# V of batch 0 with two tokens to a partition: odd and even keys in separate 64-row score and value matmuls

## The chip, the cores and the metric

The kernel runs on one core of one Trainium2 chip. The metric is the device time of the whole program in microseconds (us), as a median of several runs.

## The reference

Chunked attention with memory, followed by a two-layer network. There are 4 batches, 8 heads, 768 tokens and 64 elements to a head; a chunk has 32 queries, which see 16 keys to the left, their own 32 and 8 to the right, and 8 memory keys:

```python
for c in range(nc):                       # 24 chunks of 32 queries
    q_c = q[:, :, c_start:c_end]
    k_full = np.concatenate([mem_k, k[:, :, l_start:r_end]], axis=2)
    v_full = np.concatenate([mem_v, v[:, :, l_start:r_end]], axis=2)
    scores = scale * np.matmul(q_c, k_full.transpose(0, 1, 3, 2))
    a = np.exp(scores - np.max(scores, axis=-1, keepdims=True))
    a = a / (np.sum(a, axis=-1, keepdims=True) + 1e-09)
    out[:, :, c_start:c_end] = np.matmul(a, v_full)
...
x = out.transpose(0, 2, 1, 3).reshape(3072, 512)
h = x @ w_in                              # 512 -> 2048
s = np.sin(alpha * h)
return (h + s * s / (alpha + 1e-09)) @ w_out
```

## The kernel before, in words

**Tiles.** Three chunks make a block of 96 queries (QW), so a head has NJ = 8 blocks. The keys of a block are a window of 128 rows: 64 tokens from 16 before the block, 8 memory keys, 56 more tokens. Scores are computed transposed, keys on partitions and queries along the free dimension, so that exp gives the weights of the value matmul directly. A column of ones behind V gives the sum of a row; `normed` (L384) takes its reciprocal and multiplies on DVE, and `turned` (L396) transposes the result on PE, copies it on DVE or ACT and so fills xT, the input of the network. `half_tile` (L456) is the first matmul of the network (L462), `sine` (L473) its sine on ACT, `finish` (L487) the sum on DVE, `second` (L496) the second matmul (L500).

**Stages.** Stage -1, here called the front, does attention of batch 0 and nothing else. Stage i (0 to 3) does the network of batch i, with attention of batch i + 1 in between. The five strings of WORDS (L22) are a hand-kept list of words, one string to a stage, and every engine gets its instructions in the order of the words. In the front: `y`, `z` are filler matmuls on zeros; `a4A` casts a loaded piece of q or k (pieces 0 to 3 are k of two heads each, 4 to 7 q) on ACT (A) or DVE (V); `k1`, `l1` transpose k or q of two heads on PE (`turn`, L308) and `K1V`, `L1A` copy them out; `s10` computes scores of heads 2 and 3 in the first half of the sequence (`u_scores`, L348), `v10` the values (`u_values`, L373); `t10`, `T10` the turn with its copy on DVE or ACT; `V024` loads V of heads 2 and 3 of batch 0; `C` stands for constants, `m0` puts the memory values into V's tile, `I27` loads columns of w_in, `p`/`P` start the first network tile early.

**Batch 0.** A call of `u_scores` handles two heads (e = 0, 1) and four blocks. The two heads lie on partitions 0 to 63 and 64 to 127, so their matmuls have 64 rows each. Masking is added by a matmul of `mrow` and `mind` (L351) into the same PSUM banks, then eight score matmuls follow (L359, 96 columns each) and one exp on ACT (L366). `u_values` has eight matmuls (L378) of 128 rows and 65 columns. V's tile `vw` holds one token on a partition; `load_v` (L197) fetches it with 256-byte pieces in two DMAs a call, from POOL's queue (L209, L216, L205 for the first block). POOL issues its DMAs in order, as do SP (k of the first six heads, then outputs) and ACT (q of the first six heads). The memory values are cast (L827) and spread over the blocks on DVE (L225).

PE runs its instructions in order; every matmul that is printed below has a weight load (LDWEIGHTS) of its own ahead of it.

## Time and profile before

| | |
|---|---|
| median of 3 runs | 215.37 us (214.87 to 215.49) |
| the profiled execution, by the clock outside | 214.11 us |
| its span, first to last instruction | 212.0 us |
| PE busy | 203.1 us (96%) |
| DVE, ACT, POOL busy | 139.9, 142.8, 100.8 us |
| first network matmul (L462) | 23.48 us after the span's start |
| bytes moved by DMA | 27.82 MB in 95853 packets |

How to read the rows. A row of the timeline is: start, duration (both in us), engine, line, operation, out<-in, shapes, count, and in brackets how long the engine was idle before and what ended it. PE is the matmul, PEld the weight load, DVE the vector engine, ACT the scalar engine, POOL the engine that issues most loads. A name with q (ACTq, SPq) is the engine's sequencer, here with the DMAs that it issues. The busy time by windows gives for a stretch of time the busy us and the number of instructions of each engine. A row of the DMA table is queue, packets, MB, and the time of the packets as a share of 16 engines' time; an issue row ends with the us from issue to landing. "issue" as the reason of a wait means that nothing in the profile explains it.

### The profile page before, as it was taken

How to read it: one execution, taken by the hardware profiler on the slowest of the kernel's cores; microseconds unless marked ns; L12 is line 12 of the kernel's file. 1: busy time of each engine (PE TensorE's matmuls, PEld its weight loads, DVE VectorE, ACT ScalarE, POOL GpSimd, SP SyncE). 2: the span in 40 equal slices, each digit the busy share in tenths (PEclk: the TensorE clock that was granted, in tenths of full speed). 3: DMA queues.
4: the chain of work that ended last, by engine and by line, in shares of the span. 5: the costliest groups of instructions: out<-in, count | busy, mean ns of one | idle time of the engine just before them, and what ended most of it. 6: DMA issues, size and time to landing. Idle time of an engine off the chain costs nothing.

```text
span 212.0 us, 4567 instructions
## 1 busy us (share of the span) xinstructions
PE 203.1 (96%) x1759; PEld 117.6 (55%) x1781; DVE 139.9 (66%) x211; ACT 142.8 (67%) x228; POOL 100.8 (48%) x142
## 2 busy tenths in 40 slices
PE   7798899999999999999999999999999999999994
PEld 7566555655455555555456555554555555554443
DVE  4788788999352669957675659887347189964011
ACT  2698798978838479978827299878755188891110
POOL 8988607498696395119894048960000023300000
PEclk9999999999999999999999999999999999999999
DMA  5999999999999999999998259999244400000312
GB/s 163 327 156 145 209 208 204 204 164 177 151 167 128 172 128 128 103 148 147 158 186 137 68 126 125 160 173 126 103 105 108 136 0 3 2 0 0 152 49 99
DMA packets 95853, 27.82 MB, mean 131 GB/s; under 512 B 84808, under 2 KB 92376, under 8 KB 95832
## 3 DMA queue, kind: packets, MB, share of 16 engines
q0 software_dynamic: 69152, 13.64, 85.9%
q1 hardware_dynamic: 25720, 12.68, 30.3%
q10 hardware_dynamic: 960, 1.21, 1.7%
q8 instruction: 14, 0.23, 0.5%
q14 instruction: 7, 0.06, 0.1%
HBM read 29.66 MB, written 6.29 MB: 170 GB/s over the span
## 4 chain that ended last, share of the span: by engine, by line
PE 77%; DVE 8%; ACT 5%; issue 4%; DMA 3%; POOL 1%; SPq 1%; DVEq 0%
PE ps L500 39%; PE ps L462 28%; DVE gT L489 3%; DMA kq_f<-in_k_dram 3%; PE ps L448 3%; DVE s L485 3%; PE ps L419 2%; ACT u L477 2%; DVE x_blk L388 2%; PE ps L313 1%; PE ps L400 1%; ACT qT L333 1%; POOL s L485 1%; ACT s L482 1%; PE ps L359 1%
## 5 line engine op out<-in xcount | busy, mean ns | idle before, releaser
L500 PE MATMUL ps<-w_out_sb,gT 128*128 128x512 bf16 (+2 forms) x382 | 86.9, 370 | 1.3 <-issue 0.3
L462 PE MATMUL ps<-xT,w_in_sb 128*128 128x384 bf16 x512 | 86.4, 326 | 0.6 <-DVE gT L489 0.3
L489 DVE SCALAR_TENSOR_TENSOR gT<-s,inv_alpha,ps 128x768 bf16<-128x768 f32 x64 | 63.1, 1012 | 11.9 <-POOL s L485 5.3
L462 PEld LDWEIGHTS <-w_in_sb 128*128 128x128 bf16 x512 | 49.6, 98 | 35.5 <-issue 2.3
L477 ACT ACTIVATE u<-ps,alpha_sb 128x768 f32<-128x768 f32 x64 | 56.6, 894 | 18.2 <-PE ps L462 17.9
L500 PEld LDWEIGHTS <-gT 128*128 128x128 bf16 x400 | 36.6, 98 | 37.8 <-DVE gT L489 0.2
L485 POOL TENSOR_TENSOR s<-u 128x768 f32<-128x768 f32 x11 | 17.9, 1632 | 65.5 <-ACT u L477 54.5
L433 ACT ACTIVATE pt<-ps,biasm 128x256 bf16<-128x256 f32 x72 | 27.1, 488 | 10.5 <-PE ps L419 10.5
L507 DVE COPY o_sb<-ps 128x512 f32<-128x512 f32 (+1 forms) x15 | 10.1, 678 | 28.4 <-PE ps L500 26.5
L485 DVE TENSOR_TENSOR s<-u 128x768 f32<-128x768 f32 x24 | 22.9, 953 | 7.3 <-ACT u L477 7.3
L482 ACT ACTIVATE s<-u 128x768 f32<-128x768 f32 x29 | 24.2, 841 | 0.5
L388 DVE TENSOR_TENSOR x_blk<-ps,rinv 96x512 bf16<-96x512 f32 x32 | 22.0, 687 | 1.1
L507 ACT COPY o_sb<-ps 128x512 f32<-128x512 f32 (+1 forms) x10 | 5.6, 561 | 22.3 <-PE ps L500 22.3
L387 DVE RECIPROCAL rinv<-ps 96x8 f32<-96x8 f32 x32 | 6.4, 199 | 13.4 <-PE ps L448 12.7
L209 POOL DMA_DIRECT2D vw<-in_v_dram x13 | 11.9, 912 | 6.6 <-PE ps L400 5.5
L216 POOL DMA_DIRECT2D vw<-in_v_dram x13 | 13.3, 1024 | 3.3 <-DMA vw<-in_v_dram 3.0
L275 POOL DMA_DIRECT2D kst<-in_k_dram x16 | 12.1, 758 | 1.7 <-DMA vw<-in_v_dram 0.9
L269 POOL DMA_DIRECT2D kst<-in_k_dram x16 | 11.7, 731 | 1.9 <-DMA vw<-in_v_dram 1.2
L282 POOL DMA_DIRECT2D q_bf<-in_q_dram x12 | 10.7, 911 | 0.0
L448 PEld LDWEIGHTS <-pt 128*128 128x128 bf16 x192 | 8.2, 97 | 4.2 <-ACT pt L433 0.3
L403 ACT COPY xT<-ps 128x384 bf16<-128x384 bf16 x10 | 4.9, 496 | 7.7 <-PE ps L400 7.7
L448 PE MATMUL ps<-vw,pt 128*128 128x65 bf16 x192 | 8.9, 193 | 0.0
(83 smaller groups left out, 139.0 us busy)
## 6 DMA issues: line engine op xcount, KB each, us to landing
out_dram<-o_sb SPq DMA_DIRECT2D x23, 256.0 KB, 2.7
q_bf<-in_q_dram POOLq DMA_DIRECT2D x12, 128.0 KB, 7.0
kq_f<-in_k_dram SPq DMA_DIRECT2D x3, 384.0 KB, 6.0
kq_f<-in_q_dram ACTq DMA_DIRECT2D x3, 384.0 KB, 8.5
w_in_sb<-in_moe_w_in_dram POOLq DMA_DIRECT2D x1, 1152.0 KB, 12.6
vw<-in_v_dram POOLq DMA_DIRECT2D x7, 128.0 KB, 7.8
vw<-in_v_dram POOLq DMA_DIRECT2D x8, 112.0 KB, 8.0
kst<-in_k_dram POOLq DMA_DIRECT2D x14, 64.0 KB, 5.9
```

Source lines behind the costliest of these rows:

```text
L216: nc.gpsimd.dma_start(vw[72:128, c0:hi, 0:D], win(vflat, base + QW * c0 + 48, hi - c0, 56))
L275: nc.gpsimd.dma_start(kst[72:72 + n, j, :].rearrange("p (h d) -> p h d", d=D), k[b, :, QW * j + 48:QW * j + 48 + n, :].rearrange("h p d -> ...
L388: nc.vector.tensor_tensor(out=x_blk[:].rearrange("p g e d -> p e g d"), in0=otv[0:QW, :, :, 0:D], in1=rinv[:].unsqueeze(3).to_broadcast([Q ...
L433: nc.scalar.activation(pt[:, 0:H * QW].rearrange("p (g e c) -> p g e c", g=2, e=4)[:, :, :, 32 * m:32 * m + 32], sc[:, :, 0:4 * QW].rearra ...
L448: nc.tensor.matmul(otv[:, e, hp, :], pt[:, QW * i:QW * i + P], vws[b % 2][:, 2 * hp + e, j, 0:D + 1],)
L462: nc.tensor.matmul(t["hT"][:, hf, 0:HALF], w_in_sb[:, kt, P * t["ft"]:P * t["ft"] + P], t["xT"][:, kt, HALF * hf:HALF * hf + HALF], start= ...
L477: nc.scalar.activation(t["u"][:], t["hT"][:, :, 0:HALF], ACTF.Sin, scale=alpha_sb[:, ft:ft + 1])
L482: nc.scalar.activation(s2[:], u[:], ACTF.Square)
L485: e.tensor_tensor(out=s2[:], in0=u[:], in1=u[:], op=ALU.mult)
L489: nc.vector.scalar_tensor_tensor(out=gT[:, ft, :].rearrange("p (e c) -> p e c", e=2), in0=t["s2"][:], scalar=inv_alpha[:, ft:ft + 1], in1= ...
L500: nc.tensor.matmul(o[:, c0:c1], gT[:, ft, P * s:P * s + P], w_out_sb[:, ft, c0:c1], start=(ft == 0), stop=(ft == FT - 1),)
L507: copier(state["engines"][state["o"] % len(state["engines"])])(o_sb[:, c0:c1], o[:, c0:c1])
```

## The change

V of batch 0 is stored with two consecutive tokens on one partition, and two neighbouring blocks (ab = 0, 1) lie side by side: one on partitions 0 to 63, the other on 64 to 127. In a block of 64 partitions, 32 hold the first 64 tokens, 4 the 8 memory keys, 28 the last 56 tokens; the 64 + 64 + 1 columns are the even tokens, the odd tokens, and the ones. `load_v0` loads with 512-byte pieces in four DMAs a call (five for the first heads). Scores are computed for even (r = 0) and odd (r = 1) keys apart, 64 keys at a time, and the values add up three matmuls of 64 rows: odd keys with the ones, even keys, even keys with the ones again for the row's sum. The two blocks of a pair use different rows of the array and different PSUM banks.

Memory values: two small casts on DVE and eight DMAs from SP (`put_memv0`) in place of one cast and one DVE copy. The mask's column is built from sums of the identity in another layout (`const_c`), and the bias columns of the later batches (`const_b`) and the ones of the later V tiles (`const_w`) move to stage 0. The words of the front are reordered: fewer fillers (`y`, `z`), two of ACT's copies of k and q go to DVE (`K1V`, `L1V`), one load of V for heads 4 to 7 in place of two.

```diff
@@ WORDS, front
-        'y1 y1 y1 Ci y1 a4A We y1 Cb a1A y1 y2 y1 y1 dq068 Cl y1 Cm y1 Cf z1 z1 eVA z1 eVA a0A Ck m0 Cz z1 '
-        'dk068 Cp V024 l0 L0A k1 V002 k0 a5V y1 V068 K0A s01 y1 z1 a2V y1 Cv K1A l1 L1A s00 k2 s10 a6V s11 k3 '
-        'V046 l3 K2V K3V v10 l2 dm L3A L2A v11 s31 T10 z1 v01 s30 v00 y1 s20 I02 t01 v30 s21 T11 v31 Cs z1 '
-        'v20 T30 T00 v21 I27 t31 t20 p0 Ws t21 P0 '
+        'y1 Cc y1 y1 z1 z1 Ci eVA z1 y1 y1 We Cl a4A a0A y2 dq068 Ck y1 Cf z1 y1 a1A Cv Cm a5V Cz m0 dk068 z1 '
+        'y1 Cp V024 V002 l0 k0 y1 k1 V048 K1V L0A l1 K0A s01 s00 y1 a2V L1V k2 eVA s10 dm s11 a6V k3 K2V K3V '
+        'l2 l3 L3A L2A v10 v11 s31 I02 Cs v01 s20 s30 t10 v00 T11 T01 v31 v30 s21 v20 T00 T30 v21 T31 t20 y1 '
+        'Ws p0 t21 P0 I27 '
@@ stage 0: 'g15 f7 h14' is followed by 'Cb Cw' ahead of 'V125'
@@ load_v0 (new, called by load_v for batch 0)
+        for ab in range(2):
+            lo = 4 * h0
+            if lo == 0 and ab == 0:
+                nc.gpsimd.dma_start(vw[8:32, 0:1, 0:2 * D], rows_of(0, 1, 24))
+                lo = 1
+            nc.gpsimd.dma_start(vw[64 * ab:64 * ab + 32, lo:4 * h1, 0:2 * D],
+                                rows_of(QW * (2 * lo + ab) - 16, 4 * h1 - lo, 32))
+            nc.gpsimd.dma_start(vw[64 * ab + 36:64 * ab + 64, 4 * h0:4 * h1, 0:2 * D],
+                                rows_of(QW * (8 * h0 + ab) + 48, 4 * (h1 - h0), 28))
@@ put_memv0 (new)
+        for p0 in (32, 96):
+            for j in range(4):
+                nc.sync.dma_start(
+                    v0[p0:p0 + 4, :, j, 0:2 * D],
+                    memv_st[32:36, 0:2].rearrange("n a (h r) d -> n (a h) (r d)", r=2)
+                )
@@ u_scores
-        for i in range(4):
-            j = 4 * half + i
-            for e in range(2):
-                nc.tensor.matmul(
-                    t[:, e, QW * i:QW * i + QW],
-                    kTs[b % 2][64 * e:64 * e + 64, hp, 104 * j:104 * j + P],
-                    qTs[b % 2][64 * e:64 * e + 64, hp, QW * j:QW * j + QW],
-                    start=False, stop=(i == 3),
-                )
+        for c in range(4):
+            r, jp = c // 2, c % 2
+            for ab in range(2):
+                j = 4 * half + 2 * jp + ab
+                for e in range(2):
+                    nc.tensor.matmul(
+                        t[64 * ab:64 * ab + 64, e, QW * c:QW * c + QW],
+                        kTs[b % 2][64 * e:64 * e + 64, hp, 104 * j:104 * j + P].rearrange(
+                            "p (k r) -> p k r", r=2)[:, :, r],
+                        qTs[b % 2][64 * e:64 * e + 64, hp, QW * j:QW * j + QW],
+                        start=False, stop=(c == 3),
+                    )
@@ u_values
-        for e in range(2):
-            for i in range(4):
-                nc.tensor.matmul(
-                    otv[:, e, i, :], pt[:, HALF * e + QW * i:HALF * e + QW * i + P],
-                    vws[b % 2][:, 2 * hp + e, 4 * half + i, 0:D + 1],
-                )
+        for jp in range(2):
+            for e in range(2):
+                i = 2 * jp + e
+                vv = v0[:, 2 * hp + e, 2 * half + jp, :]
+                for r, o0, o1, c0 in ((1, 0, D + 1, D), (0, 0, D, 0), (0, D, D + 1, 2 * D)):
+                    c = HALF * e + QW * (2 * r + jp)
+                    for ab in range(2):
+                        rows = slice(64 * ab, 64 * ab + 64)
+                        nc.tensor.matmul(
+                            otv[:, ab, i, o0:o1], pt[rows, c:c + P], vv[rows, c0:c0 + o1 - o0],
+                            start=(r == 1), stop=(o0 == D),
+                        )
@@ const_f
-        nc.vector.tensor_copy(memv_st[64:72, 0], memv_f[64:72])
+        for a in range(2):
+            nc.vector.tensor_copy(memv_st[32:36, a].rearrange("n h d -> n (h d)"), memv_f(a))
```

What that makes of PE's queue, at the first value block of the front. Before, `v10` follows the transposes of q and goes on to eight pairs of a weight load and a matmul (pt2 is the weights after exp, vw0 is V):

```order
L313 LDWEIGHTS q_bf_107
L313 MATMUL ps_75<-ident_76,q_bf_107 64x128
L378 LDWEIGHTS pt2_98
L378 MATMUL ps_75<-vw0_88,pt2_98 128x65
L378 LDWEIGHTS pt2_98
L378 MATMUL ps_75<-vw0_88,pt2_98 128x65
```

In the changed kernel the same block begins like this, and goes on to 24 pairs:

```order
L416 LDWEIGHTS pt2_99
L416 MATMUL ps_75<-vw0_89,pt2_99 128x65
L416 LDWEIGHTS pt2_99
L416 MATMUL ps_75<-vw0_89,pt2_99 128x65
L416 LDWEIGHTS pt2_99
L416 MATMUL ps_75<-vw0_89,pt2_99 128x64
L416 LDWEIGHTS pt2_99
L416 MATMUL ps_75<-vw0_89,pt2_99 128x64
L416 LDWEIGHTS pt2_99
L416 MATMUL ps_75<-vw0_89,pt2_99 128x1
L416 LDWEIGHTS pt2_99
L416 MATMUL ps_75<-vw0_89,pt2_99 128x1
```

Two matmuls (blocks ab = 0 and 1) stand for each of the three parts, and each has its own weight load, also where the next one loads the same weights. From the program's start to the first network matmul, PE has 698 instructions before and 1054 after.

DVE's queue in the front, from the memory values to the first casts of q and k. Before (memv_f, memk_f are the loaded memory values and keys, kq_f the loaded pieces of q and k):

```order
L827 CAST memv_st_104<-memv_f_123 8x512
L812 CAST memv_st_104<-memk_f_122 16x512
L820 COPY memkT_108<-ps_75 128x64
L244 COPY kT0_84<-memkT_108 128x4x8x8
L244 COPY kT1_85<-memkT_108 128x4x8x8
L225 COPY vw0_88<-memv_st_104 8x64x64
L691 TENSOR_TENSOR q_bf_107<-kq_f_119 128x768
L691 TENSOR_TENSOR k_bf_106<-kq_f_116 128x768
```

And in the changed kernel:

```order
L875 CAST memv_st_105<-memk_f_123 16x512
L883 COPY memkT_109<-ps_75 128x64
L273 COPY kT0_85<-memkT_109 128x4x8x8
L273 COPY kT1_86<-memkT_109 128x4x8x8
L891 CAST memv_st_105<-kq_f_118 4x512
L891 CAST memv_st_105<-kq_f_122 4x512
L861 COPY mrow_79<-ps_75 128x128
L734 TENSOR_TENSOR q_bf_108<-kq_f_120 128x768
L353 COPY kT0_85<-ps_75 128x8x2x48
L734 TENSOR_TENSOR k_bf_107<-kq_f_117 128x768
L362 COPY qT0_87<-ps_75 128x768
```

The copy of the memory values into V (L225) has left DVE, the mask's row (mrow) is copied later, and a copy of k and one of q stand between the casts.

## The prediction

> **What bounds the kernel now.** I read the page's busy table first, then the windows by stage, then the timeline of the front, the part before the first matmul of stage 0. The busy table, and the busy time by windows (PE, PEld, DVE, ACT, POOL with counts, then clock, DMA share, GB/s):

> ```profile
> PE 203.1 (96%) x1759; PEld 117.6 (55%) x1781; DVE 139.9 (66%) x211; ACT 142.8 (67%) x228; POOL 100.8 (48%) x142
> 24.00:75.00 51.00, 50.30 (x472) 29.00 (x477) 35.68 (x50) 37.74 (x63) 31.91 (x40) 1.00 1.63 175
> 75.00:212.00 137.00, 132.82 (x946) 72.95 (x957) 85.82 (x113) 88.21 (x142) 47.12 (x52) 1.00 0.93 103
> ```

> From 24 us on PE is busy for 50.30 of 51.00 and 132.82 of 137.00 us. The change leaves those matmuls alone, so what it is worth is how much earlier or later stage 0 starts; a delay there can win back at most the 0.70 us of PE idle time up to 75 us. The front ends with a DVE chain into the first sine:

> ```profile
> 16.07 0.69 DVE L388 TENSOR_TENSOR x_blk<-ps,rinv 96x512 bf16<-96x512 f32 x1
> 22.31 0.41 PE L378 MATMUL ps<-vw,pt 128*128 128x65 bf16 x8
> 23.24 0.69 DVE L388 TENSOR_TENSOR x_blk<-ps,rinv 96x512 bf16<-96x512 f32 x1
> 23.85 0.88 DVE L403 COPY xT<-ps 128x384 bf16<-128x384 bf16 x3
> 25.18 0.90 ACT L477 ACTIVATE u<-ps,alpha_sb 128x768 f32<-128x768 f32 x1 [0.78 <-PE ps L462]
> ```

> The last value matmuls are at 22.31, the first sine at 25.18. DVE normalizes eight blocks between 15.84 and 23.9 with little idle time, so DVE, not V's arrival, sets the end now. One row does not fit that: a PE stall with no releaser.

> ```profile
> 16.03 0.40 PE L378 MATMUL ps<-vw,pt 128*128 128x65 bf16 x7
> 16.94 0.20 PE L378 MATMUL ps<-vw,pt 128*128 128x65 bf16 x1 [0.52 <-issue]
> 16.93 0.10 PEld L378 LDWEIGHTS <-pt 128*128 128x128 bf16 x1 [0.64 <-issue]
> ```

> The eighth matmul of a block, whose operands are those of the seven before it, and its weight load start 0.7 us late. "issue" says that nothing in the profile holds them. I read it as missing program code. The page's DMA table and the counts around the stall:

> ```profile
> q8 instruction: 14, 0.23, 0.5%
> 0.00:10.25 10.25, 7.87 (x94) 6.56 (x96) 6.38 (x26) 4.36 (x6) 9.31 (x34) 1.00 0.81 245
> 10.25:16.93 6.68, 5.82 (x128) 4.25 (x128) 5.74 (x8) 6.24 (x10) 6.13 (x10) 1.00 2.67 157
> 16.93:24.03 7.10, 6.35 (x125) 4.90 (x128) 6.28 (x16) 6.28 (x10) 6.41 (x10) 1.00 2.09 171
> ```

> Queue q8 brings 0.23 MB of instructions in 14 packets, and PE has 1759 + 1781 = 3540: 65 bytes each, 253 to a packet. Between 10.25 us and the stall lie 128 + 128 = 256 instructions; the next 256 (with missing records) end at 24.03. So PE's code comes in blocks of 256, with borders at 10.25, 16.93 and 24.03. The packets, by the queue table of three narrow windows (13.8 to 15.4, 19.8 to 21.1, 27.6 to 28.7 us):

> ```profile
> q8 instruction: 1, 0.02, 5.8%
> q8 instruction: 1, 0.02, 5.5%
> q8 instruction: 1, 0.02, 5.3%
> ```

> Share times 16 engines times window gives 1.48, 1.14 and 0.93 us for one packet. Each fits its window with 0.1 to 0.2 us to spare, so they end near 15.3, 21.0 and 28.6 us, and begin 2.9 to 3.7 us after the borders at 10.25, 16.93 and 24.03. The picture: entering a block asks for the next one, and PE holds no more. What was asked for at 10.25 was usable at 16.93, 6.7 us later and 1.6 us after its packet ended. Asked for at 16.93, the next should have been usable at 21.0 + 1.6 = 22.6 (5.7 us), and the one asked for at 24.03 at 30.2 (6.2 us); PE needed them later, so nothing showed. **In the front PE cannot run more than 256 instructions in 5.7 to 6.7 us**; before, it ran just under that. [...]

> **The change part by part.** (a) *More PE instructions.* Each score call goes from 10 matmuls to 18, each value call from 8 to 24, every one with its own weight load: 8 x (8 + 16) = 192 matmuls, 384 instructions. Ten filler pairs go (-20). In the order of the program, the first stage-0 matmul is instruction 698 on PE before and 1054 after. Code borders stand at the counts of the rows above: 190, 446 and 699 recorded instructions, 4 to 7 more with fillers that the trace lacks, and 256 further each. Before, two borders (194, 450) lie ahead of stage 0; after, four (194, 450, 706, 962), and the third and fourth blocks have to be fetched at the pace of DMA.

> (b) *The chain of fetches.* In the new order instruction 194 lies in the transposes of q's heads 2 and 3, which wait for a DVE cast, which waits for q:

> ```profile
> 2.13 0.51 ACTq L753 DMA_DIRECT2D kq_f<-in_q_dram  x1
> kq_f<-in_q_dram ACTq DMA_DIRECT2D x1, 384.0 KB, 7.6
> 10.61 0.96 DVE L691 TENSOR_TENSOR q_bf<-kq_f 128x768 bf16<-128x768 f32 x1
> ```

> q lands at 2.13 + 7.6 = 9.73, the cast takes 0.96: border 194 at 10.7, against 10.25. Then + 6.7 = 17.4 for block 450 (the first values cannot start before it; they were at 15.21), + 5.7 = 23.1 for block 706, + 6.2 = 29.3 for block 962. Behind that border stand two turns, the last values, two more turns, then stage 0's early matmuls. Before, last values to first sine took 25.18 - 22.31 = 2.87 us; with two turns ahead (0.35) and twelve pairs of matmuls in place of eight, less a DVE backlog that is gone, I take 3.1: sine at 32.4 against 25.18, **+7.2 us**.

> (c) *Price of a matmul.* 64-row pairs already run in the score matmuls:

> ```profile
> 12.65 0.34 PE L351 MATMUL ps<-mind,mrow 64*128 64x384 bf16 x2
> 12.82 0.33 PE L359 MATMUL ps<-qT,kT 64*128 64x96 bf16 x8
> ```

> Two of 384 columns take together what one does, eight of 96 columns about 0.13 us beyond one duration of 203 ns: pairs in different rows overlap. Values become 12 pairs in place of 8 single matmuls of some 32 ns: +0.1 us a call if pairs overlap, +0.5 if not (24 x 32 ns); scores +0.05 to +0.3. All of it lies inside the waits for code, which leave PE idle for 3 us and more per block. I take 0; if that cover is gone it costs 1.2 to 6.4 us of PE time, partly in 1.6 us of idle time (6.68 + 7.10 - 5.82 - 6.35).

> (d) *V's DMAs.* 13 in place of 9, with half the packets.

> ```profile
> L209 POOL DMA_DIRECT2D vw<-in_v_dram x4: 826/844/927, 6.1 to 13.3; - x4
> DMA to landing us min/median/max: 6.8/7.5/8.3
> 12.17 0.87 POOL L216 DMA_DIRECT2D vw<-in_v_dram  x1 [0.34 <-DMA q_bf<-in_q_dram]
> ```

> V lands 7.5 us after issue, the last at about 21, and POOL's ninth load waits for the first to land: eight are in flight at most. Issues get shorter (562 ns for the small one, 844 for the large) but more numerous, so POOL is done with V at 16 to 17 in place of 15.05, and V lands at 16 to 19. Heads 4 to 7 are read behind border 706, at 23 and later: hidden either way. w_in's pieces are issued 1 to 2 us later but find the queue emptier; stage 0 starts 7 us later: 0.

> (e) *DVE, ACT, SP.* Two DVE operations go and two small casts come:

> ```profile
> 6.61 0.58 DVE L827 CAST memv_st<-memv_f 8x512 bf16<-8x512 f32 x1
> 9.36 1.22 DVE L225 COPY vw<-memv_st 8x4096 bf16<-8x4096 bf16 x1
> ```

> -0.58 - 1.22 + 2 x 0.58 = -0.6 us on DVE. Two of ACT's copies go to DVE. All of it is idle beside the code waits: 0. The eight SP loads of memory values have nothing behind them until the first output. Of biasm, eight small DVE operations move to stage 0 (about 1.1 us there, and two POOL memsets), beside PE's matmuls: 0 to +0.5, I take +0.3; what stage 0 recovers of its 0.70 us of waits I take as -0.6.

> **Sum:** 7.2 + 0.3 - 0.6 = +6.9 us. The profiled execution took 214.11 us by the clock outside (span 212.0), 1.26 below the median of the three runs, 215.37. So 221.0 for a run like it, and against the median **222.3 us**. Bounds of the fetch chain: border 194 at 10.3 and fetches of 6.0, 5.2 and 5.5 us give +4.5; fetches of 6.7 each and border at 11 give +9.

> **The rivals.**
> 1. *Code stays ahead* (not slower). If PE's store is larger than I read it, or fetch is quicker with V's packets halved, the front stays DVE's: from q's landing at 9.73, seven operations of some 0.88 us bring DVE to 15.9, eight normalizations of 0.86 and three copies of 0.3 to 23.7, against 24.73 now: -0.8 at the sine with PE's part, +0.2 in stage 0: -0.6, **214.8 us**. For it: one stall of 0.5 us in a whole run. Against it: its place exactly on a border of 256. It decides when a block is there within about 3 us of the border before it. [...]
> 2. *Code stays ahead, and pairs do not overlap.* PE gets 8 x 0.39 for values and 8 x 0.26 for scores, 5.2 us; 1.5 us of fillers and 1.6 us of idle time absorb 3.1: +2.1, **217.4 us**.
> 3. *Code waits, and the PE clock drops.* At the start PE ran slow:

> ```profile
> PEclk9999999999999999999999999999999999999999
> 1.20 4.45 PE L730 MATMUL ps<-zeros 128*128 128x128 bf16 x40 [1.20 <-DVE tiny L767]
> 11.43 0.84 PE L730 MATMUL ps<-zeros 128*128 128x128 bf16 x8
> ```

> 40 fillers in 4.45 us are 111 ns each, 8 later ones some 80 ns (the PEclk row shows 9 in both places, so it won't tell). PE would idle for 3 to 4 us ahead of borders 706 and 962; if it falls back to the slow rate for some 4 us of work, half of that is lost: +2.2, **224.5 us**. [...]

> **How the numbers follow.** The forecast has 0.66, rival 3 0.14, rival 1 0.11, rival 2 0.05, others 0.04. Most likely: 222.3 us. The range 218.5 to 226.0 takes in the fetch chain's bounds on most of their way and rival 3: about 0.80. A measurement tells about 0.3% (0.65 us) from no change. Faster by more: half of rival 1, 0.06; within: 0.06; slower: rest, 0.88.

> **What would show it.** Right: PE "issue" waits of 2 us and more at 256-instruction borders in the front, one q8 packet shortly ahead of each; values starting at 17 or later; four borders before the first L502 matmul; first sine near 32; stages after it of the same length. Wrong: values near 15 and a first sine near 24.6 to 27 without such waits; or waits that end with V's DMAs or with DVE. If the sine is late but "issue" is small, the cause is another one.

## The result, and the profile after

The changed kernel takes 222.0 us (median of four runs, 221.04 to 222.76) against 215.43 for the kernel before on the same chip: ratio 1.031, interval 1.026 to 1.035. The profiled execution took 222.76 us, with a span of 220.8; it is the slowest of the four, and the profiled execution of the kernel before (214.11) is faster than all the runs behind 215.43, so the traces differ by more (8.65 us) than the medians (6.6). The forecast was 222.3.

The busy table, the row of the granted clock, which has 40 slices of 5.52 us, and the instruction queue, from the page after:

```profile
PE 209.8 (95%) x1959; PEld 120.4 (55%) x1959; DVE 140.5 (64%) x219; ACT 142.4 (64%) x227; POOL 101.2 (46%) x145
PEclk9997559999999999999999999999999999999999
q8 instruction: 15, 0.25, 0.5%
```

PE has about 200 more matmuls on record and one more packet of code, and its clock is down to 0.7, 0.5 and 0.5 in slices 4 to 6, 16.6 to 33 us. Next the timeline of the front after (start, duration, engine, line, operation, count, and in brackets how long the engine idled and what ended it):

```profile
16.14 0.30 PE L342 MATMUL ps<-ident,q_bf 128*64 128x128 bf16 x4 [0.71 <-issue]
17.04 1.11 PE L416 MATMUL ps<-vw,pt 64*128 64x65 bf16 x47 [0.46 <-DMA vw<-memv_st]
21.72 0.30 PE L390 MATMUL ps<-qT,kT 64*64 64x96 bf16 x4 [0.94 <-issue]
28.17 0.18 PE L416 MATMUL ps<-vw,pt 64*128 64x1 bf16 x2 [1.69 <-issue]
28.29 0.82 PE L439 MATMUL ps<-ident,x_blk 96*128 96x96 bf16 x8
30.72 1.17 PE L502 MATMUL ps<-xT,w_in_sb 128*128 128x384 bf16 x3
33.29 0.90 ACT L517 ACTIVATE u<-ps,alpha_sb 128x768 f32<-128x768 f32 x1 [1.08 <-PE ps L502]
```

Three waits have no releaser. Matched with the program's order, they are at PE instructions 449/450, 705/706 and 961/962: exactly the borders of 256. Each breaks a run of like matmuls: four transposes, four score matmuls and two value matmuls are left over behind it. The first sine comes at 33.29 instead of 25.18. The busy time by windows, cut at the borders (PE, PEld, DVE, ACT, POOL, then clock, DMA share, GB/s):

```profile
10.96:16.14 5.18, 4.47 (x132) 3.07 (x129) 5.05 (x6) 3.56 (x5) 2.79 (x5) 1.00 1.29 157
16.14:21.72 5.58, 4.12 (x126) 2.70 (x127) 2.50 (x6) 3.12 (x4) 5.53 (x9) 0.74 1.37 128
21.72:28.16 6.44, 4.75 (x128) 3.71 (x127) 2.94 (x7) 2.48 (x4) 4.32 (x7) 0.50 1.12 173
28.16:36.00 7.84, 7.83 (x77) 5.52 (x78) 3.64 (x8) 5.10 (x8) 0.54 (x1) 0.73 1.16 204
```

Each of the first three windows holds about 256 PE instructions and lasts 5.18, 5.58 and 6.44 us, of which PE works 4.1 to 4.8. DVE is busy for half or less from 16 us on: it no longer sets the end. So PE's waits for code are 0.71, 0.94 and 1.69 us, 3.3 in all; from 18.8 us on its work is stretched by the clock as well. In three narrow windows (13.3 to 14.9, 19.1 to 20.2, 25.8 to 26.8 us) the queue table shows one packet of code each:

```profile
q8 instruction: 1, 0.02, 5.5%
q8 instruction: 1, 0.02, 5.1%
q8 instruction: 1, 0.02, 5.6%
```

They start 2.4, 3.1 and 4.1 us behind the border before them, at 13.39, 19.21 and 25.86, and PE goes on 2.3 to 2.8 us after each start.

From the first sine to the end of the span it takes 220.8 - 33.29 = 187.5 us, before 212.0 - 25.18 = 186.8. So 8.1 of the 8.8 us between the two spans arise in the front.

### The profile page after: what moved, and what is told of

The parts are those of the page before. It is cut to its first block, busy times and chain, and to the rows that moved or that the text cites. A ratio compares the mean times of both kernels' runs of the same rounds, so it can differ in the third digit from the quotient of the medians.

```text
span 220.8 us, 4975 instructions
## 1 busy us (share of the span) xinstructions
PE 209.8 (95%) x1959; PEld 120.4 (55%) x1959; DVE 140.5 (64%) x219; ACT 142.4 (64%) x227; POOL 101.2 (46%) x145
## 4 chain that ended last, share of the span: by engine, by line
PE 77%; DMA 7%; DVE 6%; issue 4%; ACT 3%; POOL 1%; SPq 0%; DVEq 0%; ACTq 0%
PE ps L540 38%; PE ps L502 27%; DVE gT L529 4%; DMA kq_f<-in_q_dram 4%; PE ps L488 3%; DVE s L525 2%; PE ps L459 2%; PE ps L439 2%; DMA vw<-memv_st 2%; PE ps L416 2%; DMA kq_f<-in_k_dram 2%; ACT u L517 2%; PE ps L342 1%; PE ps L390 1%; POOL s L525 1%
## 5 line engine op out<-in xcount | busy, mean ns | idle before, releaser
L540 PE MATMUL ps<-w_out_sb,gT 128*128 128x512 bf16 (+2 forms) x400 | 89.0, 371 | 0.0
L502 PE MATMUL ps<-xT,w_in_sb 128*128 128x384 bf16 x512 | 87.1, 327 | 0.6 <-DVE gT L529 0.3
L502 PEld LDWEIGHTS <-w_in_sb 128*128 128x128 bf16 x512 | 49.9, 98 | 35.7 <-issue 2.9
L547 DVE COPY o_sb<-ps 128x512 f32<-128x512 f32 (+1 forms) x15 | 10.1, 678 | 28.4 <-PE ps L540 26.5
L304 POOL DMA_DIRECT2D kst<-in_k_dram x16 | 13.3, 829 | 1.5 <-DMA vw<-in_v_dram 1.5
L298 POOL DMA_DIRECT2D kst<-in_k_dram x16 | 11.1, 694 | 1.2 <-DMA vw<-in_v_dram 0.9
L230 POOL DMA_DIRECT2D vw<-in_v_dram x9 | 8.5, 940 | 5.6 <-PE ps L439 5.6
L311 POOL DMA_DIRECT2D q_bf<-in_q_dram x12 | 10.6, 904 | 0.0
L237 POOL DMA_DIRECT2D vw<-in_v_dram x9 | 8.9, 991 | 2.1 <-DMA vw<-in_v_dram 2.1
## 6 DMA issues: line engine op xcount, KB each, us to landing
kq_f<-in_k_dram SPq DMA_DIRECT2D x3, 384.0 KB
kq_f<-in_q_dram ACTq DMA_DIRECT2D x3, 384.0 KB
```

The lines of the kernel that those rows point to most:

```text
L298: nc.gpsimd.dma_start(kst[r0:64, j, :].rearrange("p (h d) -> p h d", d=D), k[b, :, lo + r0:lo + 64, :].rearrange("h p d -> p h d"),)
L304: nc.gpsimd.dma_start(kst[72:72 + n, j, :].rearrange("p (h d) -> p h d", d=D), k[b, :, QW * j + 48:QW * j + 48 + n, :].rearrange("h p d -> ...
L502: nc.tensor.matmul(t["hT"][:, hf, 0:HALF], w_in_sb[:, kt, P * t["ft"]:P * t["ft"] + P], t["xT"][:, kt, HALF * hf:HALF * hf + HALF], start= ...
L540: nc.tensor.matmul(o[:, c0:c1], gT[:, ft, P * s:P * s + P], w_out_sb[:, ft, c0:c1], start=(ft == 0), stop=(ft == FT - 1),)
L547: copier(state["engines"][state["o"] % len(state["engines"])])(o_sb[:, c0:c1], o[:, c0:c1])
```

## The experiments

The theory is the forecast's: PE may not enter a block of 256 instructions until a fetch, asked for at the border before it, has come. The rivals are the matmuls' own time ("work"), V's transfers ("loads"), the clock, and the new order of the front. All runs, with the PE instruction number of the first product matmul in the order of the program, and the first sine and the rest of the span behind it, in us:

| kernel | number | first sine | rest | ratio to before (interval) |
|---|---|---|---|---|
| before | 698 | 25.18 | 186.8 | 1 |
| changed | 1054 | 33.29 | 187.5 | 1.031 (1.026 to 1.035) |
| e1 changed, one value matmul of three fewer | 926 | 29.85 | 188.3 | 1.019 (1.012 to 1.027) |
| e2 before, 176 short fillers | 1050 | 33.08 | 186.7 | 1.041 (1.034 to 1.050) |
| e3 before, 24 long fillers | 746 | 30.17 | 186.6 | 1.017 (1.012 to 1.023) |
| e4 changed, padded start | 1142 | 31.11 | 187.5 | 1.028 (1.021 to 1.034) |
| e5 as e4, V of four heads in one | 1141 | 36.10 | 188.6 | 1.048 (1.042 to 1.055) |
| e6 changed, V of four heads in one | 1053 | 35.44 | 188.5 | 1.045 (1.037 to 1.053) |
| e7 changed, 11 long fillers | 1076 | 35.61 | 187.4 | 1.043 (1.033 to 1.052) |
| e8 before, padded start | 762 | 25.38 | 186.6 | 0.998 (0.994 to 1.002) |
| e9 before, new order | 668 | 28.73 | 188.0 | 1.013 (1.007 to 1.019) |
| e10 before, matmuls cut in two | 953 | 33.05 | 187.0 | 1.030 (1.022 to 1.037) |
| e11 changed, old order | 1084 | 38.03 | 187.3 | 1.054 (1.047 to 1.060) |
| e12 as e9, memory values earlier | 668 | 28.05 | 187.9 | 1.011 (1.006 to 1.015) |

The first sine is that of one profiled execution each, the ratio is over all runs. The rest varies by 2 us, the first sine by 13: most of what a kernel gains or loses here lies ahead of the first sine.

### Instructions or PE time: e2 and e3

Both leave the kernel before as it is and add fillers behind each score and value call: `n7` and `n15` are 7 and 15 matmuls of one column, `z1` and `z2` one and two of 512 columns.

```diff
-  ... s01 y1 z1 a2V ... v10 l2 ...
+  ... s01 n7 y1 z1 a2V ... v10 n15 l2 ...      (e2)
+  ... s01 z1 y1 z1 a2V ... v10 z2 l2 ...       (e3)
```

> The kernel before, with one-column filler matmuls in the front: 7 behind each score block, 15 behind each value block, 176 pairs of load and matmul, so that the first network matmul is instruction 1050 on PE (698 before, 1054 in the changed kernel). V's loads, layout and all else are those of before. Theory 'code': the same four borders as in the changed kernel, waits without a releaser at 450, 706 and 962, 220 to 224 us. Theory 'work': 176 x 0.03 = 5.3 us of PE time, 1.6 of it in idle time, 218 to 219.5. Theory 'loads': 215.4.

> The control of the run with short fillers: the kernel before with 512-column filler matmuls at the same places, 1 behind each score block and 2 behind each value block: 24 x 0.215 = 5.2 us, about the same PE time, in 48 instructions in place of 352. First network matmul is instruction 746. Theory 'code': only the work, since block 706 arrives before PE gets there: 217 to 219.5, no wait without a releaser at 706, and 2 us or more below the run with short fillers. Theory 'work': equal to the run with short fillers, 218 to 219.5. Theory 'loads': 215.4 to 217.

The fillers by shape, groups of instructions of e2 and then of e3 (busy us, mean ns; three of e3's 27 are there before too):

```profile
L735 PE MATMUL ps<-zeros 128*128 128x1 bf16 x176 | 7.0, 164 | 1.3 <-issue 1.3
```

```profile
L724 PE MATMUL ps<-zeros 128*128 128x512 bf16 x27 | 8.8, 381 | 0.0
```

The long ones hold PE for longer, and yet the short ones cost 5.4 us more (224.1 against 218.7; 2.9 at the sine in the two traces, of which e2's is the fastest of its four runs). e2's timeline has the waits again, at 705/706 and 961/962, though none at 450, where one was expected; e3 has none at its borders:

```profile
22.73 0.20 PE L378 MATMUL ps<-vw,pt 128*128 128x65 bf16 x1 [0.58 <-issue]
28.54 0.28 PE L735 MATMUL ps<-zeros 128*128 128x1 bf16 x5 [1.28 <-issue]
33.08 0.90 ACT L477 ACTIVATE u<-ps,alpha_sb 128x768 f32<-128x768 f32 x1 [1.51 <-PE ps L462]
```

So the number of instructions has a price that the time of the matmuls does not explain. Not all of the 5.4 us is waiting: the two waits are 1.9 us, and e2's granted clock was down twice (a mean of 0.73 from 10.6 to 16.9 us, ahead of any wait for code, and 0.88 from 23.7 to 30.2). e3 says a second thing: where PE does not wait for code, its time in the front is not free either, 24 long fillers cost 4.2 us.

### The splitting alone: e10

```diff
-            for e in range(2):
+            for k0, e in ((0, 0), (0, 1), (64, 0), (64, 1)):
                 nc.tensor.matmul(
-                    t[:, e, QW * i:QW * i + QW],
-                    kTs[b % 2][64 * e:64 * e + 64, hp, 104 * j:104 * j + P],
+                    t[k0:k0 + 64, e, QW * i:QW * i + QW],
+                    kTs[b % 2][64 * e:64 * e + 64, hp, 104 * j + k0:104 * j + k0 + 64],
...
+                for h0 in (0, 64):
+                    c = HALF * e + QW * i + h0
                     nc.tensor.matmul(
-                        otv[:, e, i, :], pt[:, HALF * e + QW * i:HALF * e + QW * i + P],
+                        otv[h0:h0 + 64, e, i, :], pt[:, c:c + 64],
```

> The kernel before with its matmuls of batch 0 cut in two and nothing else changed: each score matmul writes its 128 keys as 64 + 64, each value matmul its outputs as 64 + 64, with V's layout, V's DMAs, the memory values and the words as they were. 128 matmuls and 256 PE instructions more, first product matmul at instruction 953 instead of 698. Theory (the number of instructions): stalls without a releaser at instructions 706 and 962, first sine at 28.0 to 31.0 us instead of 25.2, ratio 1.012 to 1.026. Rival 'work' (what costs is the matmuls' time, and halves that use other columns of the array run side by side): no such stalls, sine at 25.2 to 26.7, ratio 0.998 to 1.008.

Measured 221.81 us, 1.030: as much as the whole change, with old layout, loads, order and memory values, and with 128 added matmuls in place of 192. The timeline and two windows:

```profile
16.89 0.30 PE L313 MATMUL ps<-ident,q_bf 128*64 128x128 bf16 x4 [0.96 <-issue]
23.74 0.54 PE L359 MATMUL ps<-qT,kT 64*64 64x96 bf16 x16 [2.71 <-issue]
33.05 0.90 ACT L479 ACTIVATE u<-ps,alpha_sb 128x768 f32<-128x768 f32 x1 [1.88 <-PE ps L464]
```

```profile
16.90:23.70 6.80, 3.98 (x126) 3.02 (x128) 3.47 (x8) 3.42 (x5) 6.45 (x10) 0.90 2.17 164
23.70:30.20 6.50, 5.99 (x122) 4.77 (x123) 3.49 (x9) 3.38 (x6) 0.74 (x2) 0.50 1.13 212
```

PE waits at the borders 450 and 706; 962 falls behind the first product matmul (953) and costs nothing. The direction is the theory's, the size above its range: block 706 took 6.85 us to come (16.89 to 23.74), and behind it PE worked with 0.50 of its clock, 6.5 us for the 248 instructions to 953.

### Under the code limit: e4 and e1

e4 puts 44 one-column filler pairs at the very start, where PE has time, so that PE crosses each border 88 instructions earlier in the work of the front. e1 leaves out the third matmul of a value group, and with it the even keys' share of the row's sum.

```diff
-  'y1 Cc y1 y1 z1 z1 Ci eVA ...
+  'y1 Cc y1 y1 z1 z1 n44 Ci eVA ...            (e4)
```

```diff
-                for r, o0, o1, c0 in ((1, 0, D + 1, D), (0, 0, D, 0), (0, D, D + 1, 2 * D)):
+                for r, o0, o1, c0 in ((1, 0, D + 1, D), (0, 0, D, 0)):       (e1)
```

> The changed kernel with 44 one-column filler pairs (88 instructions) added at its very start, where PE has nothing to do: the work stands 88 instructions later against the borders, so the first border is crossed some 3 us earlier in time (near 8 in place of 10.96 us) and the last one ahead of the network lies in the last half of heads 6 and 7's values. Theory 'code': each fetch begins earlier, first sine 28.5 to 30 in place of 33.3, 218.5 us (217.5 to 220): work is added and time goes. Theory 'work': 222.0 to 223. Theory 'loads': 222.0.

> The changed kernel without the third value matmul (the even keys' share of the row's sum is left out, so rows are divided by the odd keys' sum alone): 64 one-column matmuls and their 64 weight loads fewer, and the first network matmul is instruction 926 on PE in place of 1054. Theory 'code' (PE waits for blocks of 256 instructions, borders at 194, 450, 706, 962): the border at 962 now comes 18 matmuls behind the start of the network, so one block less has to arrive ahead of stage 0; first sine near 27 in place of 33.3, 217.8 us (217 to 219). Theory 'work' (the added matmuls cost PE time by themselves): 64 x 10 to 30 ns, 0.6 to 1.9 us less than the changed kernel, 220.1 to 221.4. Theory 'loads' (values wait for V or the memory values): 222.0, unchanged.

e4 runs more instructions than the changed kernel and in its trace has the sine 2.2 us earlier, which "work" and "loads" do not give. The times do not decide it: e4's ratio, 1.028, cannot be told from the 1.031 of the changed kernel and lies above what the theory gave it (217.5 to 220 us), and e1's interval reaches into the range of "work". Both runs gain less than the theory gave them. No wait for code is left ahead of the product matmuls; another has come up, here in e4 and then in e1:

```profile
24.04 1.25 PE L416 MATMUL ps<-vw,pt 64*128 64x65 bf16 x47 [2.51 <-DMA vw<-in_v_dram]
```

```profile
22.37 0.65 PE L416 MATMUL ps<-vw,pt 64*128 64x65 bf16 x31 [0.94 <-DMA vw<-in_v_dram]
```

PE has V of heads 4 to 7 only at 24.04 us in e4, because POOL stands still until earlier loads have landed, in the changed kernel too:

```profile
12.83 0.66 POOL L216 DMA_DIRECT2D vw<-in_v_dram  x1 [3.09 <-DMA q_bf<-in_q_dram]
```

So some 2 to 3 us below the code limit lies a limit of the loads.

e1 also shows that the pace of 256 instructions is not fixed. Counted on the rows of its timeline, one block of 256 went by from 16.30 to 20.57 us, 4.3 us without a wait, where the changed kernel needed 5.18 and 5.58. A block can be there sooner, then; why it was there sooner in e1 is open.

### Fewer, larger V loads: e5 and e6

```diff
-  ... Cp V024 V002 l0 k0 y1 k1 V048 ...
+  ... Cp V004 l0 k0 y1 k1 V048 ...             (e5 with n44, e6 without)
```

> The padded changed kernel (44 one-column filler pairs at the start, so that TensorE crosses its code borders earlier), and V of heads 0 to 3 loaded with five DMAs in place of two sets of five and four: nine DMAs in all, as before the change. Theory (under the code limit lies the loads' limit: GpSimd may not issue the transfers of heads 4 to 7 before earlier ones have landed): the 2.7 us wait on a DMA at PE instruction 876 goes or falls below 0.7 us, the first sine comes at 28.3 to 29.5 us instead of 31.1, and the time falls from 220.6 to 218.2 us (217.3 to 219.3). Rival 'bytes' (V lands late because of its bytes, however many DMAs carry them): the wait stays near 2.7 us, 220.6. Rival 'work' (the added matmuls cost what they cost, waits or no waits): the wait goes but the time stays above 219.8.

> The changed kernel with the same merging of V's DMAs and no padding. Theory (code first, loads second): the stalls at PE instructions 450, 706 and 962 stay, 0.9 to 2 us each, and the time stays within 0.8 us of the changed kernel: ratio to the kernel before 1.027 to 1.034, 221.5 us beside a before of 214.9. Rival 'loads' (the transfers held back are what costs): 219.0 to 220.0, ratio 1.019 to 1.024.

Both theories fall: by their ratios the two are about 4.5 and 3 us slower than their counterparts, e4 and the changed kernel. e5's wait at V of heads 4 to 7 is gone, four others stand earlier, and a wait for code of 0.79 us is back at 962:

```profile
19.57 0.45 PE L416 MATMUL ps<-vw,pt 64*128 64x65 bf16 x12 [3.24 <-DMA vw<-memv_st]
20.79 0.46 PE L416 MATMUL ps<-vw,pt 64*128 64x65 bf16 x12 [0.76 <-DMA vw<-memv_st]
21.69 0.45 PE L416 MATMUL ps<-vw,pt 64*128 64x65 bf16 x12 [0.45 <-DMA vw<-memv_st]
22.53 0.41 PE L416 MATMUL ps<-vw,pt 64*128 64x65 bf16 x11 [0.39 <-DMA vw<-memv_st]
```

The SP transfers of the memory values, 8 KB each, land later: in e5 PE waits for them until 22.53 us, in e4 until 16.95. With V of four heads in one call POOL has more bytes under way (112 to 128 KB to a load in e6, where most of the changed kernel's first ones have 56 to 64) when its ninth load has to wait, in e6 for 2.83 us up to 12.92; small transfers then seem to queue behind them. The waits are shown, the queueing is argued: no run varied it alone.

### The clock: e7

Eleven `z1` in the code blocks between instructions 450 and 1060 of the changed kernel, to keep PE busy while it has to wait anyway:

```diff
-  k3 K2V K3V l2 l3 L3A L2A v10 v11 s31 I02 Cs v01 s20 s30 t10 v00 T11 T01 v31 v30 s21 v20
+  k3 z1 K2V K3V l2 l3 L3A L2A v10 z1 v11 z1 s31 z1 I02 Cs v01 z1 s20 z1 s30
+  t10 z1 v00 z1 T11 T01 v31 z1 v30 z1 s21 z1 v20
```

> The changed kernel with eleven 512-column fillers (22 PE instructions, 2.3 us of matmul at the full clock) spread over the code blocks between instructions 450 and 1060, so that TensorE is busy for more of the time that it must wait for code anyway. Theory (code sets when a block may begin, and the halved clock adds 2 us to the last stretch): the granted clock stays at 1.00 to 36 us, the borders are crossed at about the same times as without fillers (block 962 at 28.2, within 0.8 us), the first sine comes at 31.3 to 32.3 instead of 33.3, and the ratio falls to 1.020 to 1.027. Rival 'clock costs nothing here' (the stretch behind the last border is long for another reason): the sine at 33.3 or later, ratio 1.031 to 1.040. Rival 'work': eleven fillers cost their 2.3 us, ratio above 1.038.

The clock stayed up through borders 450 and 706. Then the wait at 962 was longer than ever, and the clock fell within it, as the timeline and the windows of e7 show:

```profile
29.93 0.45 PE L416 MATMUL ps<-vw,pt 64*128 64x1 bf16 x13 [3.41 <-issue]
```

```profile
22.00:26.00 4.00, 3.60 (x115) 2.68 (x116) 2.82 (x7) 1.68 (x4) 4.00 (x7) 1.00 0.98 134
28.00:30.00 2.00, 0.07 (x4) 0.08 (x6) 0.00 (x0) 0.00 (x0) 0.00 (x0) 0.55 1.07 200
30.00:33.00 3.00, 3.00 (x58) 2.66 (x59) 1.94 (x5) 1.60 (x4) 0.54 (x1) 0.50 1.12 210
```

PE crossed border 706 at 21.97 and had block 962 at 29.93: 7.96 us, though nothing kept PE from asking at the same time as in the changed kernel (21.72, 6.44 us). The time lies where the rival "work" had it (above 1.038), but PE stood still for 3.41 us at 962, with the fillers of that block done, so in the trace it is the late code that held it. The run does not isolate the clock's price; it shows that one and the same fetch can take 1.5 us more, and that fillers ahead of a border do not keep the clock through the wait at it. Why this one was slow stays open.

### The order: e9, e12 and e11

e9 gives the kernel before the new list of words; e12 is e9 with `m0`, the copy of the memory values, ahead of the cast of q (`a5V`); e11 gives the changed kernel the old list.

```diff
-  ... Ck y1 Cf z1 y1 a1A Cv Cm a5V Cz m0 dk068 ...      (e9)
+  ... Ck y1 Cf m0 z1 y1 a1A Cv Cm a5V Cz dk068 ...      (e12)
```

> The kernel before with the front's new order alone (the changed kernel's list of words, with the old bias constants in the place of the new ones): the matmuls, V's layout and the memory values stay as they were, and the first product matmul is PE instruction 668 instead of 698. Theory (all of the loss is the number of instructions): ratio 0.992 to 1.006, no stall at a border, first sine at 24.5 to 26.0 us. Rival 'order' (part of the loss lies in the reordered front): ratio 1.008 to 1.020, with the wait that causes it in the front's first 25 us.

> The kernel before with the new order, and the copy of the memory values on VectorE (1.78 us at 11.0 us with the new order, between the cast of q and the copy of k) moved ahead of the q cast, where the old order has it. Theory (that copy is what the new order loses): the 2.4 us wait at PE instruction 258 goes or falls below 1 us, first sine at 25.0 to 26.8 us instead of 28.7, ratio 0.995 to 1.006. Rival (another part of the new order costs it): the wait or the late sine stays, ratio 1.009 to 1.019.

> The changed kernel with the front's order of before (the old list of words, with the new mask constants, and V of heads 4 to 7 still in one call): first product matmul at instruction 1084. Theory (the number of instructions, the order next to nothing): stalls at 450, 706 and 962 as in the changed kernel, first sine at 32.5 to 35 us, ratio 1.026 to 1.040. Rival 'order' (the reordering costs the changed kernel the 2.9 us that it costs the kernel before): sine at 30 to 31.5, ratio 1.012 to 1.022.

e9 loses 2.9 us without a wait for code. A row of DVE and one of PE in its timeline show where it starts:

```profile
11.04 1.78 DVE L225 COPY vw<-memv_st 8x4096 bf16<-8x4096 bf16 x1
14.85 0.61 PE L313 MATMUL ps<-ident,k_bf 128*64 128x128 bf16 x12 [2.16 <-DVE k_bf L691]
```

With that copy moved (e12) the 2.16 us wait is gone as expected, but the sine is only 0.7 us earlier and the time does not fall: PE now waits for V, by three rows of up to 1.87 us, of which this is the last.

```profile
22.25 1.06 PE L378 MATMUL ps<-vw,pt 128*128 128x65 bf16 x16 [1.87 <-DMA vw<-in_v_dram]
```

The new list loads V of heads 4 to 7 in one call, where the old one fetches heads 6 and 7 first, and they are read first; that this is the cause was not tried alone. e11 is worse than either theory said. In the old order the ones of V (`Cv`) stand behind V's loads on POOL, and write into the tile that these fill:

```profile
21.63 0.23 POOL L912 MEMSET vw<- 128x32 bf16 x1 [4.40 <-DMA vw<-in_v_dram]
```

```profile
21.92 0.78 PE L416 MATMUL ps<-vw,pt 64*128 64x65 bf16 x24 [5.32 <-POOL vw L912]
```

So the order is no loss in the changed kernel: it costs the kernel before 2 to 3 us, and the changed kernel is 5 us slower without it. That wait for `Cv` alone is 5.32 us; the old list with `Cv` moved was not run, so the 5 us may be the price of that one word.

### A version for the kernel before: e8

```diff
-  'y1 y1 y1 Ci y1 a4A ...
+  'y1 y1 y1 n32 Ci y1 a4A ...
```

> The kernel before with 32 one-column filler pairs (64 PE instructions) among the fillers of its start, so that border 194 is crossed earlier and the block from 450 is there in time. Theory: the 0.5 us stall in the value matmuls at 16.9 us goes, the other borders cost nothing, and the time falls by 0.2 to 0.8 us (ratio 0.996 to 0.999). Rival: the chain through VectorE sets the sine all the same, ratio 0.999 to 1.002; or the 64 instructions push another border into the path, above 1.003.

The 0.5 us wait at 450 is gone, and one at the next border has come, where the kernel before had none; the sine is at 25.38:

```profile
22.03 0.30 PE L378 MATMUL ps<-vw,pt 128*128 128x65 bf16 x4 [0.70 <-issue]
```

The ratio, 0.998 (0.994 to 1.002), is no difference that can be told. No run here is faster than the kernel before.

## Why the prediction was right, point by point

**(a) Instructions.** Right. Four borders lie ahead of stage 0 instead of two, at the instructions given, and the number of instructions has a price of its own (e2 against e3, e10). I took 192 matmuls as the unit of the change; e10 needed 128 for the same loss.

**(b) The chain of fetches.** The mechanism held as far as the traces show it (a packet 2.4, 3.1 and 4.1 us behind each border, a wait of 0.71, 0.94 and 1.69 us at the next), two sizes were off and partly cancelled. Border 194 was crossed at 10.96 (10.7 forecast), and the blocks came after 5.18, 5.58 and 6.44 us (6.7, 5.7, 6.2): block 962 at 28.17 instead of 29.3, 1.1 us early. The last stretch, from there to the sine, took 5.12 us instead of 3.1, 2.0 us more. I had worked out 3.1 from the last value matmuls of before at a full clock, and here the clock was not full, as narrow windows of the profile after show:

```profile
18.00:19.00 1.00, 1.00 (x53) 0.75 (x48) 0.97 (x3) 0.32 (x1) 1.00 (x2) 0.89 1.55 151
19.00:19.50 0.50, 0.50 (x16) 0.17 (x12) 0.50 (x2) 0.49 (x1) 0.50 (x2) 0.50 1.34 146
32.00:33.00 1.00, 1.00 (x8) 0.59 (x6) 0.36 (x1) 0.20 (x1) 0.00 (x0) 0.78 1.14 195
```

A mean of 0.89 puts the drop to 0.50 at 18.8 us, one of 0.78 the return at 32.4. The kernel before has, for the same eight transposes that here took 0.82 us:

```profile
23.15 0.50 PE L400 MATMUL ps<-ident,x_blk 96*128 96x96 bf16 x8 [0.42 <-DVE x_blk L388]
```

From the first product matmul to the sine it was 1.70 us before (23.48 to 25.18) and 2.57 after (30.72 to 33.29). These 0.87 us and two such groups of transposes, 0.64 us, are 1.5 of the 2.0.

**Rival 3, the clock**, was therefore not a rival but part of the outcome. I priced it at 2.2 us on top, which is about what it took; the quicker fetches hid it in the total. That half of the time would be lost was my estimate, since the rows that I had gave 111 against 80 ns; the runs then showed a granted clock of 0.50, in the changed kernel for 13.65 us and not for some 4. One remark on it was wrong: that the row of the clock won't tell (it shows 7, 5, 5). Nor did PE idle for 3 to 4 us first: waits of 0.7 and 0.5 us at 15 to 17 us came ahead of the drop at 18.8, and from 16.00 to 18.78 PE was busy for 2.12 of 2.78 us. In e10 the clock fell 1.3 us into a single wait, which began at 21.03 us, 2.71 ahead of 23.74 (the mean of 0.82 puts the drop at 22.3):

```profile
20.70:21.70 1.00, 0.33 (x4) 0.18 (x3) 0.73 (x2) 0.21 (x1) 0.70 (x2) 1.00 1.23 191
21.70:22.70 1.00, 0.00 (x0) 0.00 (x0) 0.00 (x0) 0.00 (x0) 1.00 (x2) 0.82 1.17 196
```

The length of the spells at 0.50 goes in steps: 13.65 us in the changed kernel (18.78 to 32.44) and 6.8 in e7 (28.2 to 35.0, by the means of 0.72 and 0.66 in its windows). For the others, twice the span times what the mean clock lacks to 1 gives, to about 0.2 us, 10.1 in e10 (220.1 us at 0.977), 7.0 in e4 (218.6 at 0.984) and 3.5 in e12 (215.9 at 0.992). All lie near whole multiples of 3.4 us.

That the forecast of 222.3 meets the median of 222.0 so closely is in part luck. In the traces, on which the sum was built, the first sine came 0.9 us later than forecast (33.29 against 32.4) and the time rose by 8.65 us (214.11 to 222.76) in place of 6.9; the medians differ by 6.6. The two bounds are rounded outwards: added up like the sum itself, with the +0.3 and -0.6 of stage 0, they are +4.6 and +8.7 and not +4.5 and +9.

Two of the signs that were to show it right did not come: the waits are 0.71, 0.94 and 1.69 us and not 2 us and more, and the first value matmul ran at 16.38, ahead of 17. The place of the waits and the packets ahead of them are as forecast.

**(c) Price of a matmul.** Taking 0 held, but with far less cover than I gave it: I had PE idle for 3 us and more per block, and it worked 4.1 to 4.8 us of each and waited 0.7 to 1.7. At the clock that it had, code that is there at once would have won at most these 3.3 us of the 8.1 at the sine. The rest is made up of border 194, crossed 0.7 us later, a wait of 0.46 for a load, and PE's own work on 356 more instructions, from 18.8 us on at half clock. How much of these the late code brought about through the clock was not isolated. Rival 2 had fillers and idle time absorb 3.1 us of added PE time; e3's 24 long fillers cost 4.2 us at the sum, so less is absorbed than I said.

**(d) V's DMAs.** "Hidden either way" held only because code was later: V of heads 4 to 7 landed at up to 21.8 by the trace, instead of 16 to 19, with POOL idle for 3.1 us on its limit. e4 and e1 uncovered it at once. A wait of 0.46 us for the SP transfers of the memory values (17.04) I had not seen at all.

**(e) DVE, ACT, SP and stage 0.** DVE is idle as forecast. The rest of the span grew by 0.7 us, where I had +0.3 - 0.6. The new order, which I put at nothing, is worth 5 us to this kernel (e11; by the place of `Cv`, as far as was tried) and costs the one before 2 to 3 (e9, e12).

**Rival 1**, code stays ahead, is out as far as this front goes: the waits at the borders took 0.71, 0.94 and 1.69 us in the changed kernel, and up to 3.41 us (e7) in the others that have them.

## What to carry to other kernels

Count the instructions, not only the work, of an engine that is fed with small operations: in this front PE got 256 instructions per 4 to 8 us, so a block of nothing but small matmuls can run it dry of code whatever they compute. A wait with the reason "issue" in the middle of a run of like instructions, at a multiple of 256 from the last one, was the sign here (0.71, 0.94 and 1.69 us in the changed kernel). Each matmul that a split adds there counts twice, since its weight load is an instruction too: 192 matmuls were 384 instructions. And under the limit that binds lies the next one: padding removed the waits for code and won 2 us at the first sine of one trace, but no time that can be told, since a load that had looked hidden took over.
